# A third staging buffer for output tiles, with another table of places, in a fused attention and two-MLP kernel on one Trainium2 core

## The chip, the cores and the metric

The kernel runs as one program on one core of a Trainium2 chip. The metric is device time in microseconds (us), the median of several executions. The engines that work here are TensorE (PE, with its weight loads as PEld), VectorE (DVE), ScalarE (ACT) and GpSimd (POOL). SyncE (SP) issues most of the transfers, ScalarE the rest.

## The reference

Attention over 4 batches of 12 heads, 448 positions and 64 columns is followed by two small networks with gates made by a convolution over the positions. Everything is float32; the weights arrive as 64-bit words.

```python
# attention, (4, 12, 448, 64)
q_n, k_n = rmsnorm(q, g_q), rmsnorm(k, g_k)
scores = q_n @ k_n.T / sqrt(64); scores -= scores.max(-1)
attn = exp(scores); attn /= attn.sum(-1) + 1e-9
x = attn @ v                                  # heads joined: (4, 448, 768)
# first network, 768 -> 1024 -> 768, 3-tap convolution over positions
h = relu(x @ w_in)                            # (4, 448, 1024)
x = (h * sigmoid(conv3(h))) @ w_out
# second network, 768 -> 768 -> 768, causal 5-tap convolution
val = x @ w_val
out = (sigmoid(conv5(x)) * val) @ w_out2
```

## The kernel before

Every matrix product with float32 accuracy is made of three float16 matmuls: each operand is held as a high and a low half, and high times high, low times high and high times low are summed in PSUM. Attention goes by pairs of heads: rows of q and k are normed, split into halves and turned by transposing transfers (`qa`, `ka`), scores are made in PSUM (`ps`), the row maxima taken (`mx`), exponentials written as float32 (`p32`), split into halves (`p16`), turned again (`pt`) and multiplied with the split values (`vv`, `vm`). The networks use 448 columns per matmul, six or eight blocks of 128 rows deep. Their gates are sums over `scr` tiles on VectorE. Batches follow each other in a pipeline, so attention of a later batch runs beside the networks of an earlier one.

The weights of the second network's last product (`in_moe2_w_out_dram`; the profile leaves numbers in names out and prints `in_moe_w_out_dram`) are fetched in pieces of 128 rows as 64-bit words into slots of the general area `act`. `weight_piece` has a fetch (one transfer) and a split: one ScalarE operation and three VectorE ones that turn the words into float32 (`act<-act`), a ScalarE copy to float16 (`w2<-act`), and a subtraction on GpSimd or VectorE for the low half (`w2<-act,w2`).

An output tile is 128 positions by 384 columns: 18 matmuls (`ps<-act,w2`, in `out_tile`) fill a PSUM bank, `evac` takes the next of `NOSB` buffers `osb` in turn, ScalarE copies the bank into it with a factor, and a transfer stores it in memory. There are 28 such copies, seven for a batch, and 32 stores. Two of the `osb` buffers also serve the gains of the norm at the start (`load_g`).

The order of the instructions is not that of the code. A `Plan` object records every operation (`add`) with the engines that could do it, its dependencies, and the event time at which the code asked for it. `order` gives each a priority `first`: its event time and the length of the work behind it, weighed by `URGENT`, plus a number of the table `OFFSETS` for the event that it belongs to; the lowest goes first. `forward` then lays the operations on the engines by its own model of durations, four passes with `backward` between them, and picks the engine for those that have a choice: a store for example goes to SP's or to ScalarE's queue, a split of weights to one of two engines. `emit` issues the result, so all operations have the line of `emit` (L500) in the profile. Each engine works through its list strictly in order: an instruction that waits holds all those behind it on that engine, and a transfer that SP cannot issue yet holds the transfers behind it.

Of the kernel before, what the change touches and what calls it, by code (L numbers as in the profile page):

```python
# [503 lines left out]
def kernel(  # L504
# [28 lines left out]
    NT = B * S  # L533
    KC = 4
    KR = S // KC
    NQ = 4 * FULL + 2
    NKA = 2
    NV = 4
    NOSB = 2
    NP32 = 2  # L540
    NP = 2
    NTK = 1
    NTQ = 1
    NSCR = 4
    NX16 = 1
# [1357 lines left out]
```

## Time and profile before

| what | value |
|---|---|
| three executions | 618.48, 616.82, 614.95 us; median 616.82 |
| profiled execution | 614.43 us, span 612.6 us |
| granted TensorE clock, mean over the span | 0.997 |
| busy: PE, DVE, ACT, POOL | 588.7 (96%), 483.8 (79%), 413.8 (68%), 270.8 (44%) us |
| chain that ended last, share by engine | PE 70%, DVE 14%, ACT 5%, DMA 4%, issue 3%, POOL 2% |
| bytes moved, mean | 82.09 MB, 134 GB/s |

The span runs from the first to the last instruction of the trace; the profiled execution is 1.8 us longer. All times in the rows below count from the span's start. The share of busy time is a mean over the span, and the stretches of it have different limits, so rows are read by stretch.

### The profile page before, as it was taken

How to read it: one execution, taken by the hardware profiler on the slowest of the kernel's cores; microseconds unless marked ns; L12 is line 12 of the kernel's file. 1: busy time of each engine (PE TensorE's matmuls, PEld its weight loads, DVE VectorE, ACT ScalarE, POOL GpSimd, SP SyncE). 2: the span in 40 equal slices, each digit the busy share in tenths (PEclk: the TensorE clock that was granted, in tenths of full speed). 3: DMA queues.
4: the chain of work that ended last, by engine and by line, in shares of the span. 5: the costliest groups of instructions: out<-in, count | busy, mean ns of one | idle time of the engine just before them, and what ended most of it. 6: DMA issues, size and time to landing. Idle time of an engine off the chain costs nothing.

```text
span 612.6 us, 12783 instructions
## 1 busy us (share of the span) xinstructions
PE 588.7 (96%) x4747; PEld 344.4 (56%) x4747; DVE 483.8 (79%) x1145; ACT 413.8 (68%) x796; POOL 270.8 (44%) x301
## 2 busy tenths in 40 slices
PE   5989899998999999899999999999999999999997
PEld 2767686554666554455555556555455565555554
DVE  6899998989999998898699884499997743397720
ACT  4978999998879986796567663878775543263221
POOL 2254746675556865577375751636661200000000
PEclk9998999999999999999999999999999999999999
DMA  8772758887638879986977867956665675000002
GB/s 207 182 174 62 215 174 205 175 185 170 148 102 226 162 160 166 204 197 105 213 137 144 148 130 181 167 108 112 124 96 111 105 140 119 14 1 1 1 13 78
DMA packets 230803, 82.09 MB, mean 134 GB/s; under 512 B 216863, under 2 KB 226645, under 8 KB 230741
## 3 DMA queue, kind: packets, MB, share of 16 engines
q1 hardware_dynamic: 229413, 79.51, 61.9%
q10 hardware_dynamic: 1328, 1.77, 1.2%
q8 instruction: 37, 0.61, 0.4%
q14 instruction: 25, 0.20, 0.1%
HBM read 38.59 MB, written 5.51 MB: 72 GB/s over the span
## 4 chain that ended last, share of the span: by engine, by line
PE 70%; DVE 14%; ACT 5%; DMA 4%; issue 3%; POOL 2%; SPq 1%; DVEq 0%; ACTq 0%; POOLq 0%
PE ps L500 70%; DVE act L500 3%; DVE w L500 3%; DVE ps L500 3%; DMA act<-in_moe_w_out_dram 2%; DVE scr L500 2%; ACT act L500 1%; DVE half L500 1%; DVE ssq L500 1%; ACT p L500 1%; DMA w<-in_moe_w_out_dram 1%; DMA ka<-tk 1%; SPq L500 1%; DVE root L500 1%; ACT w L500 1%
## 5 line engine op out<-in xcount | busy, mean ns | idle before, releaser
L500 DVE TENSOR_SCALAR_CACHE_REDUCE ps<-ps,root 128x448 f32<-128x448 f32 x168 | 109.4, 687 | 24.6 <-PE ps L500 23.4
L500 PE MATMUL ps<-act,wo 128*128 128x448 f16 x576 | 123.1, 353 | 1.1 <-DVE act L500 1.1
L500 PE MATMUL ps<-act,wi 128*128 128x448 f16 x576 | 117.9, 353 | 4.1 <-DVE scr L500 2.4
L500 ACT ACTIVATE p<-ps,mx 128x448 f32<-128x448 f32 x154 | 91.3, 633 | 27.6 <-DVE mx L500 11.8
L500 POOL TENSOR_TENSOR p<-p,p 128x896 f16<-128x896 f32 x40 | 76.5, 1915 | 65.5 <-ACT p L500 51.7
L500 PE MATMUL ps<-act,wv 128*128 128x448 f16 x432 | 90.3, 353 | 0.3 <-DVE act L500 0.3
L500 PE MATMUL ps<-w,act 128*128 128x384 f16 (+1 forms) x576 | 88.5, 326 | 0.4 <-ACT osb L500 0.4
L500 PEld LDWEIGHTS <-wo 128*128 128x128 f16 x576 | 55.6, 99 | 52.5 <-issue 8.2
L500 PEld LDWEIGHTS <-wi 128*128 128x128 f16 x576 | 54.1, 98 | 54.3 <-issue 8.5
L500 PE MATMUL ps<-ka,qa 64*128 64x448 f16 (+3 forms) x512 | 81.1, 418 | 0.8 <-ACT ka L500 0.7
L500 PE MATMUL ps<-vv,pt 128*128 128x65 f16 (+5 forms) x1440 | 80.0, 205 | 0.2 <-ACT pt L500 0.2
L500 ACT ACTIVATE act<-ps 128x448 f16<-128x448 f32 (+4 forms) x89 | 46.8, 532 | 42.1 <-DVE ps L500 21.9
L500 PEld LDWEIGHTS <-act 128*128 128x128 f16 (+1 forms) x576 | 48.5, 101 | 33.4 <-issue 5.0
L500 PEld LDWEIGHTS <-wv 128*128 128x128 f16 x432 | 40.5, 98 | 38.8 <-issue 4.6
L500 DVE SCALAR_TENSOR_TENSOR act<-ps,cw,act 128x446 f32<-128x446 f32 (+3 forms) x96 | 62.0, 674 | 0.3
L500 PEld LDWEIGHTS <-pt 128*128 128x128 f16 (+1 forms) x1344 | 51.4, 101 | 17.5 <-issue 6.4
L500 ACT ACTIVATE p<-p 128x896 f16<-128x896 f32 x56 | 53.4, 953 | 0.5
L500 DVE SCALAR_TENSOR_TENSOR w<-w 128x768 uint32<-128x768 uint32 (+1 forms) x56 | 47.1, 846 | 0.1
L500 DVE SCALAR_TENSOR_TENSOR scr<-ps,cw,scr 128x447 f32<-128x447 f32 x64 | 41.7, 675 | 1.2 <-ACT scr L500 0.8
L500 DVE SCALAR_TENSOR_TENSOR act<-ps,act 128x448 f16<-128x448 f32 x48 | 29.6, 619 | 6.5 <-ACT act L500 6.4
L500 ACT ACTIVATE osb<-ps 128x384 f32<-128x384 f32 x28 | 13.6, 491 | 30.6 <-PE ps L500 23.7
L500 ACT ACTIVATE ps<-ps 128x448 f32<-128x448 f32 x32 | 16.5, 538 | 25.3 <-PE ps L500 25.3
(131 smaller groups left out, 914.2 us busy)
## 6 DMA issues: line engine op xcount, KB each, us to landing
w<-in_moe_w_in_dram SPq DMA_DIRECT2D x8, 768.0 KB, 6.1
w<-in_moe_w_out_dram SPq DMA_DIRECT2D x8, 768.0 KB, 5.0
kin<-in_k_dram SPq DMA_DIRECT2D x24, 224.0 KB, 3.8
qin<-in_q_dram SPq DMA_DIRECT2D x36, 128.0 KB, 3.4
act<-in_moe_w_out_dram SPq DMA_DIRECT2D x12, 384.0 KB, 4.3
w<-in_moe_w_val_dram SPq DMA_DIRECT2D x12, 384.0 KB, 3.3
vst<-in_v_dram SPq DMA_DIRECT2D x16, 224.0 KB, 3.6
out_dram<-osb SPq DMA_DIRECT2D x17, 192.0 KB, 2.2
```

The lines of the kernel that those rows point to most:

```text
L500: getattr(getattr(nc, e), method)(*a, **k)
```

## The change

`NOSB` goes from 2 to 3, so that the copies of output tiles take three buffers in turn. The table `OFFSETS` is replaced by a longer one with other numbers. Nothing is computed differently: the 6842 recorded operations are the same.

```diff
 OFFSETS = {
...
+    33: -3.36, 38: 0.13, 40: 0.12, 41: 0.12, 42: 0.12, 43: 0.12, 49: 0.56, 56: -0.57, 59: 4.29, 60: 0.25, 61: -2.33, 62:
+    0.25, 63: 0.25, 82: 0.32, 93: -0.21, 94: -0.21, 97: -1.15, 102: 1.97, 106: 0.29, 107: -0.72, 112: -1.3, 115: -5.28,
...
 }
...
     NKA = 2
     NV = 4
-    NOSB = 2
+    NOSB = 3
     NP32 = 2
```

The third buffer shifts by one the numbers behind the names of tiles made later (`ps_116` before is `ps_117` now, `mx2_102` is `mx2_103`). The instructions of both orders stand at the same places, but for swaps over a few places, up to about 238 us of the run before. Behind that they differ on every engine, and both the table and the third buffer have a part in that. VectorE has 977 operations before and 970 now, ScalarE 806 and 810, SP issues 307 transfers and now 311, the matmuls are the same ones.

The first place is ScalarE at 238 us. The rows are its list, before and now; `act_82<-act_82` is a weight piece in conversion, `p32_0` holds the exponentials of scores.

```order
L500 ACTIVATE mx2_102<-mx2_102 128x2
L500 ACTIVATE rs1_110<-ps_116 128x6
L500 ACTIVATE act_82<-act_82 128x384
L500 ACTIVATE p32_0_88<-ps_116,mx2_102 128x448 x2
L500 ACTIVATE p32_1_89<-ps_116,mx3_103 128x448
L500 ACTIVATE p16_0_90<-p32_0_88 128x896
```
```order
L527 ACTIVATE mx2_103<-mx2_103 128x2
L527 ACTIVATE rs1_111<-ps_117 128x6
L527 ACTIVATE vv3_73<-vst1_79 128x7x64
L527 ACTIVATE p32_0_88<-ps_117,mx2_103 128x448 x2
L527 ACTIVATE act_82<-act_82 128x384
L527 ACTIVATE p16_0_90<-p32_0_88 128x896
```

The conversion of the weight piece stood ahead of the exponentials and now stands behind them; the split of a value tile (`vv3`) came to its place.

The second place is VectorE at 249 to 257 us. `scr` are the gate sums of the first network, and the row `scr2_96<-scr2_96,ps_116` (now `ps_117`) is the product of a finished gate with its PSUM tile.

```order
L500 SCALAR_TENSOR_TENSOR scr2_96<-ps_116,cw1_113,scr2_96 128x447
L500 TENSOR_SCALAR act_82<-act_82 128x384
L500 SCALAR_TENSOR_TENSOR scr2_96<-ps_116,cw1_113,scr2_96 128x447
L500 SCALAR_TENSOR_TENSOR scr0_94<-ps_116,cw1_113,scr0_94 128x447
L500 SCALAR_TENSOR_TENSOR scr1_95<-ps_116,cw1_113,scr1_95 128x447
L500 SCALAR_TENSOR_TENSOR scr2_96<-scr2_96,ps_116 128x448
L500 SCALAR_TENSOR_TENSOR act_82<-act_82 128x384
```
```order
L527 SCALAR_TENSOR_TENSOR scr2_96<-ps_117,cw1_114,scr2_96 128x447
L527 SCALAR_TENSOR_TENSOR scr0_94<-ps_117,cw1_114,scr0_94 128x447
L527 SCALAR_TENSOR_TENSOR scr2_96<-ps_117,cw1_114,scr2_96 128x447
L527 SCALAR_TENSOR_TENSOR scr0_94<-ps_117,cw1_114,scr0_94 128x447
L527 SCALAR_TENSOR_TENSOR scr1_95<-ps_117,cw1_114,scr1_95 128x447
L527 SCALAR_TENSOR_TENSOR scr2_96<-scr2_96,ps_117 128x448
```

The conversions of the weight piece (`act_82<-act_82`) left the place ahead of that product.

SP's list at the same time: transfers that turn tiles, and weight pieces from memory.

```order
L500 DMA_TRANSPOSE pt0_92<-p16_0_90 128x14x128
L500 DMA act_82<-in_moe2_w_out_dram 128x768
L500 DMA_TRANSPOSE pt1_93<-p16_1_91 128x14x128
L500 DMA_TRANSPOSE ka1_67<-tk0_86 128x8x112
L500 DMA act_82<-in_moe2_w_out_dram 128x768
```
```order
L527 DMA_TRANSPOSE pt0_92<-p16_0_90 128x14x128
L527 DMA_TRANSPOSE ka1_67<-tk0_86 128x8x112
L527 DMA_TRANSPOSE pt1_93<-p16_1_91 128x14x128
L527 DMA act_82<-in_moe2_w_out_dram 128x768 x2
L527 DMA kin1_84<-in_k_dram 112x8x64
```

The turning of keys (`ka1`) and of probabilities (`pt1`) now stands ahead of the weight piece that was between them. ScalarE's operation that converts this piece moved with it, to seven places further back.

The third place is SP at 268 to 283 us: the last two weight pieces.

```order
L500 DMA act_82<-in_moe2_w_out_dram 128x768
L500 DMA_TRANSPOSE act_82<-x16_0_80 128x3x128
L500 DMA_TRANSPOSE pt0_92<-p16_0_90 128x14x128
L500 DMA_TRANSPOSE act_82<-x16_0_80 128x3x128
L500 DMA act_82<-in_moe2_w_out_dram 128x768
L500 DMA_TRANSPOSE pt1_93<-p16_1_91 128x14x128
L500 DMA out_0_dram<-osb0_98 128x384
```
```order
L527 DMA_TRANSPOSE act_82<-x16_0_80 128x3x128 x2
L527 DMA_TRANSPOSE pt0_92<-p16_0_90 128x14x128
L527 DMA out_0_dram<-osb0_98 128x384
L527 DMA act_82<-in_moe2_w_out_dram 128x768
L527 DMA_TRANSPOSE pt1_93<-p16_1_91 128x14x128
L527 DMA act_82<-in_moe2_w_out_dram 128x768
L527 DMA vst0_78<-in_v_dram 128x7x64
```

Both weight pieces moved back: the first behind three turning transfers and a store, the last behind the turning of probabilities `pt1`.

## Rows read from the trace of the kernel before

**Rows 1.** Windows: us busy, instructions of PE, PEld, DVE, ACT, POOL; clock, DMA.
```profile
240.00:270.00 30.00, 27.89 (x213) 14.84 (x211) 25.63 (x54) 25.11 (x51) 19.40 (x17) 1.00 0.92 191
270.00:300.00 30.00, 29.55 (x286) 16.87 (x284) 24.22 (x56) 18.80 (x40) 21.59 (x19) 1.00 0.83 167
...
360.00:390.00 30.00, 30.00 (x301) 17.73 (x294) 16.32 (x47) 16.97 (x33) 11.15 (x10) 1.00 0.81 175
...
570.00:600.00 30.00, 30.00 (x170) 16.49 (x169) 12.89 (x22) 6.30 (x12) 0.00 (x0) 1.00 0.04 14
```
**Rows 2.** Chain that ended last, its end: start us, us, what.
```profile
291.31 117.58 PE ps L500 x1056
...
508.12 101.07 PE ps L500 x661
...
609.25 0.49 ACT osb L500
```
**Rows 3.** Tile osb: its instructions, and waits at it (us, times).
```profile
L500 ACT ACTIVATE osb<-ps x28: 469/491/515, 270.6 to 609.3; 128x384 f32<-128x384 f32 x28
...
  DMA out_dram<-osb: 6.8, 3
...
  ACT p L500: 2.4, 1
```
**Rows 4.** Timeline of PE: start, us, instruction, count, idle before and releaser.
```profile
239.71 3.19 PE L500 MATMUL ps<-act,wi 128*128 128x448 f16 x16 [1.33 <-ACT p L500]
...
254.49 0.35 PE L500 MATMUL ps<-act,wi 128*128 128x448 f16 x1 [1.77 <-DVE scr L500]
...
261.05 1.48 PE L500 MATMUL ps<-act,wi 128*128 128x448 f16 x7 [0.34 <-DVE scr L500]
...
287.71 3.15 PE L500 MATMUL ps<-w,act 128*128 128x384 f16 x20
291.31 0.97 PE L500 MATMUL ps<-w,act 128*128 128x384 f16 x5 [0.45 <-ACT osb L500]
```
**Rows 5.** Timeline of ACT, 238 to 258 us.
```profile
238.59 0.54 ACT L500 ACTIVATE act<-act 128x384 f32<-128x384 f32 x1 [0.77 <-DMA act<-in_moe_w_out_dram]
239.04 1.67 ACT L500 ACTIVATE p<-ps,mx 128x448 f32<-128x448 f32 x3
...
251.18 0.55 ACT L500 ACTIVATE act<-act 128x384 f32<-128x384 f32 x1 [1.28 <-DMA act<-in_moe_w_out_dram]
...
257.43 0.58 ACT L500 ACTIVATE scr<-scr 128x448 f32<-128x448 f32 x1
```
**Rows 6.** Timeline of DVE, 249 to 259 us.
```profile
251.77 0.36 DVE L500 TENSOR_SCALAR act<-act 128x384 uint32<-128x384 uint32 x1 [1.28 <-ACT act L500]
...
258.04 0.62 DVE L500 SCALAR_TENSOR_TENSOR scr<-scr,ps 128x448 f32<-128x448 f32 x1 [0.30 <-ACT scr L500]
```
**Rows 7.** Timeline of SP's queue, 246 to 283 us.
```profile
246.88 1.07 SPq L500 DMA_DIRECT2D act<-in_moe_w_out_dram  x1
...
250.27 1.67 SPq L500 DMA_TRANSPOSE ka<-tk  x1
...
275.90 0.34 SPq L500 DMA_DIRECT2D act<-in_moe_w_out_dram  x1
280.96 1.54 SPq L500 DMA_TRANSPOSE pt<-p  x1
```
**Rows 8.** Timeline of DVE, 282 to 288 us.
```profile
283.11 1.87 DVE L500 TENSOR_TENSOR half<-half,ssq 128x30 f32<-128x30 f32 x1
...
287.23 0.18 DVE L500 TENSOR_TENSOR half<-half,ssq 128x30 f32<-128x30 f32 x1
287.34 0.56 DVE L500 SCALAR_TENSOR_TENSOR act<-act 128x384 uint32<-128x384 uint32 x1
```
**Rows 9.** Timeline of ACT, 279 to 288 us.
```profile
279.77 0.54 ACT L500 ACTIVATE act<-act 128x384 f32<-128x384 f32 x1
...
287.93 0.52 ACT L500 ACTIVATE w<-act 128x384 f16<-128x384 f32 x1 [4.19 <-DVE act L500]
```

195 rows, old and new, of the table OFFSETS are left out of this document.

## The prediction

> **What bounds the kernel now.** I read the busy time by engine first, and then did not trust it: PE is busy 96% of the span, but a mean over stages hides where the other 4% lie. The windows come next [rows 1]. In 240 to 270 us PE works 27.89 of 30 us, in 270 to 300 us 29.55, and in the windows at 360 and at 570 us all 30. The chain that ended last says the same from the other end [rows 2]: from 291.31 us on its pieces are PE alone (the first has 1056 matmuls in 117.58 us, the last 661 in 101.07), up to the last copy of an output tile at 609.25. So behind 291 us the kernel is as long as its matmuls, and a change of order can only add to it; ahead of 291 us there is idle time of PE that an order could take away. The diff and the lists leave everything ahead of about 238 us as it was. What is left are four gaps of PE between 238 and 292 us [rows 4]: 1.33 us behind an exponential, 1.77 and 0.34 behind gate products of VectorE, 0.45 behind a copy of an output tile. Together 3.89 us, 0.6% of 614.43: this is all that the change can win on PE's own path, unless matmuls of the same set ran faster in another sequence.
>
> **The third buffer.** ScalarE waits for an `osb` buffer to be stored three times, 6.8 us, and an exponential once behind such a wait, 2.4 us [rows 3]; 9.2 us of waiting is what a third buffer could remove. They lie near 380 and 600 us, in the two windows where PE worked 30.00 of 30 us [rows 1]. PE did not feel them: other banks were free and other matmuls ready. So I cost the third buffer at nothing; the cover is PE's queue of matmuls, and if it were gone the wait itself, 2 to 3 us each time, would be the price. The copies of output tiles run from 270.6 us on [rows 3], so of the four gaps only the last one can have to do with them. The Trainium skill's page "Trainium Kernel Development and Optimization", section Best Practices, asks for double buffers so that transfers run beside computing. By that rule, read as "one more buffer where a buffer is waited for", the 9.2 us would come out as time; the window rows show PE without a gap there, so the trace speaks against that here.
>
> **The first place, ScalarE at 238 us.** Before, the conversion of a weight piece starts at 238.59 after 0.77 us of waiting for its transfer, and the exponentials queue behind it until 239.04; PE waits for them until 239.71 [rows 4, 5]. Now a split of a value tile, which waits for no transfer, stands there, and takes about as long as the conversion did (0.54). The exponentials start earlier by the wait, 0.77. Of the 1.33 us gap 0.77 goes. Bounds: 0, if the split has a wait that the trace doesn't show, and 1.33.
>
> **The second place, VectorE at 251 us.** Before, the conversion of a weight piece on VectorE waits 1.28 us for ScalarE, which itself waited 1.28 us for the transfer [rows 5, 6], and the gate product behind it is what PE waits 1.77 us for [rows 4]. Now the conversion stands behind the product, so this gap goes, and the one of 0.34 at 261.05 with it: 2.11. But SP's list is changed too, and here something is given back. The piece was issued at 246.88 and ScalarE could convert it at 251.18, 4.30 later. Now two turning transfers go first; the later of them ended at 250.27 + 1.67 = 251.94 before [rows 7], behind the piece's own 1.07, so the piece is issued at 251.94 - 1.07 = 250.87 and can be converted at 255.17. On ScalarE five instructions, the conversion among them, then stand ahead of the next tanh of a gate (`scr<-scr`, 257.43 before). Instructions of this kind follow each other every 0.45 us (238.59 to 239.04), so the tanh comes at 255.17 + 5 x 0.45 = 257.42, as late as before, and the gate product behind it, at 258.04 before, no earlier [rows 5, 6]. Queued behind the waiting conversion are the gates, and PE waits for them. A new wait of about 2.1 us takes the place of the old one. I keep the 0.34 of the gap at 261.05, since the conversions that stood ahead of that product are now in the wait. So the two places give between 0.34 (the gates hold PE again) and 0.77 + 2.11 = 2.88 (they don't); I take 0.77 + 0.34 = 1.1, near the lower end.
>
> **The third place, SP at 276 us.** The last weight piece was issued at 275.90; now it stands behind the turning of probabilities, which SP issued at 280.96 and held for 1.54 [rows 7], because its source came late. So the piece goes out at 282.5, 6.6 us later. With the 4.30 above it can be converted at 286.8. Then come ScalarE's 0.54 [rows 9], three operations of VectorE of 0.36 to 0.56 (1.48 together) [rows 6, 8] and ScalarE's copy of 0.52: ready at 289.3. Before, it was ready at 287.93 + 0.52 = 288.45 [rows 9], and the run of 20 matmuls at 287.71 [rows 4] went straight through, so PE had no time to spare behind it. That is 0.9 us later than before. The turning itself moves up with the 0.3 to 1.1 us won ahead of it, so against before the piece is 0.6 late at most, and 0.2 early at best. ScalarE's copy of an output tile, for which PE waited 0.45 at 291.31, is now due while PE waits for the weight, so those 0.45 are absorbed.
>
> On VectorE the same subtraction on 30 columns took 1.87 us at 283.11 and 0.18 at 287.23 [rows 8]; the stretch has long GpSimd instructions. The Trainium skill, "SBUF — State Buffer", section on two separate sides, says VectorE and GpSimd share a pair of ports as an exclusive lock, the loser blocked for the whole instruction. By it, the three moved VectorE operations could each be stretched; the sum above takes the short ones.
>
> **Behind 291 us.** The lists differ here too, and I cannot follow every place. PE has no gap, so there is nothing to win. What a wrong place can cost is bounded by a stretch that has gaps: 30 - 27.89 = 2.11 us in one window [rows 1]. I take 0 and keep 2.11.
>
> **The sum.** If the last piece comes in time, the gain is 1.1 + 0.45 = 1.55; if it is late, PE is where the piece lets it be: 0.6 late less the absorbed 0.45, a loss of 0.15 that can grow to 0.6 where the 0.45 is not absorbed. Between -1.55 and +0.6 I take -0.5. The profiled execution took 614.43 (span 612.6), so 613.9 for one like it. The median of the three runs, 616.82, is 2.4 above that execution; the change should shift both alike: 616.3.
>
> **The rivals.**
> 1. All gaps go: the late weight pieces land in the shadow of other work, and PE is gap-free from 238 us on. 616.82 - 3.89 = 612.9. For it: every one of the four gaps has its cause moved in the lists. Against it: the piece at 250 us and the last piece stand later on SP, by 4 and 6.6 us.
> 2. Slower: the last weight piece decides. Its VectorE operations fall beside GpSimd's long instructions, and one is stretched by 1.87 - 0.18 = 1.69, nothing of the earlier gain survives, and the piece is ready 0.9 + 1.69 = 2.6 late, with PE idle for it; 616.82 + 2.6 = 619.4. If the copy of an output tile that is queued on ScalarE behind the conversion then holds a PSUM bank as well, add the 0.45 again: 619.9. It decides from the point where the copy to `w` ends after 288.45 by more than what PE has won. For it: it was ready just in time before. Against it: two of the three VectorE rows there are short ones [rows 8].
> 3. The third buffer does pay: ScalarE's 9.2 us come out, 607.6. Against it is the full PE in both windows.
> 4. Nothing happens: the gains at 238 and 251 us are given back to the last tenth, 616.8. It lies inside the forecast's range.
>
> **How the numbers follow.** Forecast 0.53 (rival 4 included), all gaps gone 0.25, slower by the last piece or a place behind 291 us 0.20, third buffer 0.02. A change of 0.5%, 3.1 us, is about what a measurement of this kernel can tell from none, so faster means under 613.7 and slower over 619.9. Faster: most of the second case (0.22 of 0.25) and the third buffer, 0.24. Slower: half of the 0.20 and a little of the forecast's own tail, 0.12. Same: 0.64. The forecast's own range, with half of the runs' spread (614.95 to 618.48) about it, is 614.5 to 618.2. The range of 8 in 10 takes in the other two: from just below 612.9 to 619.8.
>
> **What would show it right or wrong.** PE's gap at 239 us is shorter by 0.77. The gap at 254 us is gone, and a new one of about 2 us stands near 256 to 258 behind VectorE's gate product, which itself follows a ScalarE conversion waiting for a piece of `w_out`. Near 288 us PE waits for ScalarE's copy `w<-act`. ScalarE's waits for `osb` fall from 6.8 us to near 0 without a change in PE's windows. Wrong would be: a gap-free PE from 238 to 292 us (rival 1), several gaps behind 291 us, or another rate of matmuls in the windows where PE is full.

## The result, and the profile after

The changed kernel takes 620.23 us (median of 10 runs, 613.58 to 629.21), the kernel before 615.39 (10 runs beside it, 613.07 to 619.07). The ratio is 1.0065, with a 95% interval of 1.0039 to 1.0091: slower by 0.65%, just above the range that was forecast, and on the other side of its middle. The forecast started from 616.82, the median of three of these ten runs of the kernel before. The longest run of the changed kernel was a disturbed one and is left out of the ratio.

The timeline of PE in the changed kernel: start, duration, instruction, count, and in brackets the idle time before it with what ended it. These are all the gaps behind 238 us that the profile marks, to be read against [rows 4].

```profile
240.46 3.56 PE L527 MATMUL ps<-act,wi 128*128 128x448 f16 x18 [0.37 <-ACT p L527]
...
259.82 0.76 PE L527 MATMUL ps<-ka,qa 64*64 64x448 f16 x6 [1.60 <-DVE scr L527]
...
271.81 1.32 PE L527 MATMUL ps<-ka,qa 64*128 64x448 f16 x6 [1.87 <-DVE x L527]
...
296.01 0.34 PE L527 MATMUL ps<-vm,pt 128*128 128x130 f16 x3 [0.70 <-DMA pt<-p]
```
```profile
357.66 0.54 PE L527 MATMUL ps<-act,wv 128*128 128x448 f16 x2 [0.17 <-DVE act L527]
...
522.10 0.35 PE L527 MATMUL ps<-vm,pt 128*128 128x130 f16 x3 [0.24 <-DMA pt<-p]
```

The gap behind the exponential fell from 1.33 to 0.37 us, and the ones at 254 and 261 us are gone. Two new ones stand at 259.82 and 271.81, 1.60 and 1.87 us. The second is where the forecast had none. Its releaser is the `x` tile of VectorE. The timelines of VectorE and of GpSimd at that place:

```profile
268.39 0.55 DVE L527 CAST x<-ps 128x384 f16<-128x384 f32 x1
268.85 2.44 DVE L527 SCALAR_TENSOR_TENSOR act<-act 128x384 uint32<-128x384 uint32 x1
271.21 0.55 DVE L527 TENSOR_TENSOR x<-ps,x 128x384 f16<-128x384 f32 x1
```
```profile
268.49 0.55 POOL L527 TENSOR_SCALAR act<-act 128x384 f32<-128x384 f32 x1
268.99 1.88 POOL L527 TENSOR_TENSOR p<-p,p 128x896 f16<-128x896 f32 x1
```

A weight conversion of VectorE (`act<-act`, 384 columns) lasts 2.44 us. An instruction of this form takes 0.56 in [rows 8]. It stood beside the end of a short GpSimd instruction and beside the split of probabilities behind that, which lasted until 270.87, and the second half of the `x` tile that PE needs stood behind it. Over the whole program the instructions of this form became longer, as the lines grouped by form show, first of the kernel before, then of the changed one (busy us, mean ns of one):

```profile
L500 DVE SCALAR_TENSOR_TENSOR act<-act 128x384 uint32<-128x384 uint32 x24 | 15.1, 638 | 1.4 <-POOL act L500 1.4
```
```profile
L527 DVE SCALAR_TENSOR_TENSOR act<-act 128x384 uint32<-128x384 uint32 x24 | 20.0, 837 | 0.6 <-POOL act L527 0.4
```

The 24 instructions of this form need 4.9 us more; 1.88 of them are this one's. Behind the gap the clock fell too. Windows of 2 us of the changed kernel (us busy of PE, PEld, DVE, ACT, POOL; then the granted clock, DMA share, GB/s):

```profile
270.00:272.00 2.00, 0.19 (x2) 0.10 (x2) 2.00 (x3) 0.70 (x3) 0.95 (x2) 1.00 0.39 73
272.00:274.00 2.00, 2.00 (x9) 0.70 (x7) 2.00 (x7) 1.90 (x4) 1.56 (x3) 0.72 0.32 66
274.00:276.00 2.00, 2.00 (x6) 0.73 (x5) 2.00 (x5) 1.78 (x4) 1.75 (x3) 0.50 0.63 124
276.00:278.00 2.00, 2.00 (x26) 1.34 (x25) 2.00 (x4) 1.42 (x3) 0.78 (x1) 0.93 1.01 235
```

PE worked 0.19 of 2 us, and in the next 4 us it was granted 0.72 and 0.50, that is the lower of its levels (1.2 of 2.4 GHz) for most of them. In the window 270 to 300 us of before the clock was 1.00 [rows 1].

The account of the two profiled executions: the span grew from 612.6 to 617.6, by 5.0 us. The matmuls behind the first gap start at 240.46 against 239.71, 0.75 later although their gap is 0.96 shorter, so 1.7 us of the 5.0 were lost ahead of the first place that the change touches. They belong to that execution: its clock was 0.89 from 60 to 90 us, which is 3.3 us, while the trace of before has 0.94 from 30 to 60 us, 1.8 us. 3.3 us of the 5.0 are left. The gaps behind 238 us add up to 0.37 + 1.60 + 1.87 + 0.70 + 0.17 + 0.24 = 4.95 us against 3.89: 1.1. From 270 to 300 us the mean clock was 0.94, which is 30 x 0.06 = 1.8 us:

```profile
270.00:300.00 30.00, 27.48 (x254) 15.48 (x253) 25.42 (x52) 19.71 (x40) 20.34 (x20) 0.94 0.66 136
```

That makes 2.9 of 3.3; 0.4 us I could not place.

### The profile page after: what moved, and what is told of

Same layout as the page of the kernel before. It is cut to its first block, busy times and chain, and to the rows that moved or that the text cites. A ratio compares the mean times of both kernels' runs of the same rounds, so it can differ in the third digit from the quotient of the medians.

```text
span 617.6 us, 12804 instructions
## 1 busy us (share of the span) xinstructions
PE 592.0 (96%) x4747; PEld 346.1 (56%) x4747; DVE 487.2 (79%) x1138; ACT 416.9 (68%) x804; POOL 270.1 (44%) x300
## 4 chain that ended last, share of the span: by engine, by line
PE 63%; DVE 15%; ACT 8%; DMA 8%; issue 3%; POOL 2%; SPq 0%; ACTq 0%; DVEq 0%; POOLq 0%
PE ps L527 63%; DVE act L527 4%; DVE ps L527 4%; ACT p L527 2%; DMA pt<-p 2%; DVE w L527 2%; ACT act L527 2%; DMA ka<-tk 1%; DMA act<-in_moe_w_out_dram 1%; DMA w<-in_moe_w_in_dram 1%; DVE ssq L527 1%; ACT w L527 1%; DMA w<-in_moe_w_out_dram 1%; DVE half L527 1%; DVE tq L527 1%
## 5 line engine op out<-in xcount | busy, mean ns | idle before, releaser
L527 PE MATMUL ps<-act,wi 128*128 128x448 f16 x576 | 119.8, 356 | 0.7 <-ACT p L527 0.4
L527 DVE SCALAR_TENSOR_TENSOR act<-ps,cw,act 128x444 f32<-128x444 f32 (+3 forms) x96 | 63.1, 675 | 0.6
L527 DVE SCALAR_TENSOR_TENSOR w<-w 128x768 uint32<-128x768 uint32 (+1 forms) x56 | 45.4, 817 | 0.1
L527 PEld LDWEIGHTS ps<-vv,pt 128*128 128x128 f32 (+1 forms) x288 | 33.6, 185 | 1.2 <-issue 0.7
L527 PE MATMUL ps<-vm,pt 128*128 128x130 f16 (+3 forms) x240 | 28.5, 238 | 4.8 <-ACT pt L527 3.8
```

Of the source, the lines that this page charges most:

```text
L527: getattr(getattr(nc, e), method)(*a, **k)
```

## The experiments

Each kernel was timed in five rounds beside the kernel before. Those that move instructions do it behind the planner, on its finished lists, and nothing else changes. The numbers in `MOVES` are places in the planner's record of operations:

```diff
+    # (x, y, s): x goes right behind (s = 1) or ahead of (s = 0) y, on y's engine
+    MOVES = [...]
     def emit(self, nc):
```

**nosb3_old**, the third buffer with the old table.

```diff
-    NOSB = 2
+    NOSB = 3
```

> The third buffer with the old table. In its lists the stretch from 238 to 283 us (the split of a value tile ahead of the exponentials, the weight pieces behind the turning transfers, the weight conversion ahead of the x tile on VectorE) stands as in the changed kernel. Theory A, the loss comes from that stretch: the long VectorE act<-act of about 2.4 us beside GpSimd's p<-p,p near 270 us, a PE gap of 1.5 to 2 us behind it, a lower granted clock for some us after it; time as the changed kernel or worse, 619 to 622. Theory B, the loss comes from the new numbers of the table behind 291 us: this kernel is as fast as the one before, 614 to 617.

**nosb2_new**, the new table with two buffers: the changed kernel with

```diff
-    NOSB = 3
+    NOSB = 2
```

> Two buffers with the new table. Its lists from 238 to 283 us are nearly those of the kernel before: the x tile on VectorE is ahead of the weight conversion, the weight pieces on SP are early. Theory A: no PE gap above 1 us near 270 us, no fall of the clock there, 614 to 617. Theory B (the numbers of the table are the loss): 619 to 621.

Measured: 625.76 us, ratio 1.0175 (1.0131 to 1.0219), and 628.68 us, ratio 1.0205 (1.0168 to 1.0243). Both halves of the change are worse than the whole, and neither theory has it right: the gap near 270 us, by which they were to be told apart, is in neither. With the old table VectorE has the conversion at the same place of its list as the changed kernel, but there it takes 0.76 us and PE waits 0.20; with the new table alone PE waits 0.17. Each has gaps that the two full kernels lack. The largest of the old table with three buffers is 1.67 us, at 283.75; that of the new table alone:

```profile
419.28 6.95 PE L527 MATMUL ps<-act,wi 128*128 128x448 f16 x27 [3.93 <-DVE act L527]
```

The gaps behind 238 us add up to 6.90 and 10.40 us. What they have above the 3.89 of the kernel before is under a third of the one loss and about half of the other; the rest I did not place. Buffers and table do not add up: the planner lays its lists by dependencies, a third buffer takes some away, and the lists shift from 238 us on, 32 us ahead of the first copy of an output tile [rows 3]. Each table does worse with the other's number of buffers.

**x_first**, the weight conversion that took 2.44 us goes behind the `x` tile and two gate products.

```diff
+    MOVES = [(2499, 2857, 1)]
```

> The changed kernel with one VectorE instruction moved: the weight conversion that took 2.44 us at 268.85 goes behind the x tile and the two gate products that follow. Theory A: the x tile is done by 269.6 instead of 271.76, the PE gap of 1.87 us at 271.81 shrinks to under 0.4, and the clock does not fall at 273 us, which saves about 1.6 us more; 620.2 becomes 616 to 617.5. If the gap goes but the clock falls all the same, 618.5. If the gap is only handed on to the next weight tile, no change, 620.

Measured: 620.26 us, ratio 1.0055 (1.0019 to 1.0091). The gap of 1.87 us is gone, but the time is not won. The profile shows a loss again 85 us later. First PE, then VectorE, then GpSimd:

```profile
353.13 0.35 PE L547 MATMUL ps<-act,wv 128*128 128x448 f16 x1
356.78 0.54 PE L547 MATMUL ps<-act,wv 128*128 128x448 f16 x2 [3.30 <-DVE act L547]
```
```profile
345.95 4.19 DVE L547 TENSOR_SCALAR ssq<-ssq 128x30 f32<-128x30 f32 x1
```
```profile
345.55 1.15 POOL L547 TENSOR_TENSOR tq<-tq 128x448 f32<-128x448 f32 x1
346.64 1.90 POOL L547 TENSOR_TENSOR p<-p,p 128x896 f16<-128x896 f32 x1
348.48 1.02 POOL L547 TENSOR_TENSOR vv<-vst,vv 128x448 f16<-128x448 f32 x1
349.43 1.55 POOL L547 TENSOR_TENSOR tq<-tq 128x224 f32<-128x224 f32 x3
```

An operation on 30 columns of sums of squares (`ssq<-ssq`, called the 30-column sum below) stays 4.19 us on VectorE, from 345.95 to 350.14, while GpSimd works without a pause through three instructions into a fourth. PE then waits 3.30 us. In the changed kernel's own profile the same operation, at 350.03, takes 0.99 us, and PE waits 0.17 behind it, at 357.66. The clock falls again behind the long wait:

```profile
354.00:356.00 2.00, 0.00 (x0) 0.00 (x0) 1.86 (x9) 1.87 (x5) 0.00 (x0) 1.00 1.05 198
...
358.00:360.00 2.00, 2.00 (x13) 0.92 (x10) 1.84 (x8) 0.58 (x1) 0.00 (x0) 0.52 0.56 123
360.00:362.00 2.00, 2.00 (x24) 1.41 (x22) 0.67 (x5) 1.88 (x3) 1.30 (x2) 0.63 1.01 190
```

**pool_late**, GpSimd's split of probabilities goes behind the next low half of a weight; VectorE's list is that of the changed kernel.

```diff
+    MOVES = [(3057, 2501, 1)]
```

> The changed kernel with one GpSimd instruction moved: the split of probabilities (p<-p,p, 1.88 us at 268.99) goes behind the following low half of a weight. VectorE's list is untouched. Theory A, the conversion is long because the GpSimd instruction runs beside it: VectorE's act<-act near 269 us takes 0.55 to 0.7 us instead of 2.44, and the PE gap falls as in the run with the moved conversion; 616 to 618. Rival, VectorE's instruction is long for another reason (its source comes late): it stays at 2.4 us and the time at 620.

Measured: 618.65 us, ratio 1.0042 (1.0011 to 1.0072). VectorE and GpSimd at the place:

```profile
268.25 0.78 DVE L547 SCALAR_TENSOR_TENSOR act<-act 128x384 uint32<-128x384 uint32 x1
268.95 0.54 DVE L547 TENSOR_TENSOR x<-ps,x 128x384 f16<-128x384 f32 x1
```
```profile
268.07 0.55 POOL L547 TENSOR_SCALAR act<-act 128x384 f32<-128x384 f32 x1
...
270.83 1.89 POOL L547 TENSOR_TENSOR p<-p,p 128x896 f16<-128x896 f32 x1
```

The conversion takes 0.78 us with its own list unchanged, since GpSimd's split now starts at 270.83. So the long conversion is GpSimd's doing. This run too has the 4.2 us sum near 347 us and a PE gap of 3.38 us behind it, which eats the gain.

**ssq_pool**, the sum on 30 columns goes to GpSimd, where the kernel before has it.

```diff
+    MOVES = [(4061, 4649, 1)]
```

> The changed kernel with one operation on another engine: a sum on 30 columns (ssq<-ssq), which took 0.99 us on VectorE at 350.03 in its profile and 4.19 us in the run with the x tile first, goes to GpSimd, where the kernel before had it. Theory A (VectorE loses to GpSimd's long instructions at two places, 269 and 346 us): the gap behind VectorE's act near 357 us never appears, the one at 271 us stays; 618 to 620. Rival, the place at 346 us was an accident of the moved instructions: 620, as the changed kernel.

Measured: 617.31 us, ratio 1.0026 (0.9993 to 1.0058). The gap at 271 us stayed (1.98 us); PE's list has none near 357 us. The interval overlaps that of the changed kernel, so this run alone does not show that the sum costs anything there.

**x_and_ssq**, both edits.

```diff
+    MOVES = [(2499, 2857, 1), (4061, 4649, 1)]
```

> Both edits: the weight conversion behind the x tile, and the 30-column sum on GpSimd. Theory A: neither the gap of 1.87 us at 271.8 nor the one of 3.30 at 356.8 is left, and the clock does not fall behind them; what is left is the 1.2 to 1.6 us at 259 us; 615 to 616.5. Rival, the time lost is handed on again to a third place: 618 or more.

Measured: 616.73 us, ratio 1.0013 (0.9979 to 1.0047). Its profile has neither a gap behind the `x` tile nor one near 357 us. With both places mended the kernel cannot be told from the one before. The intervals of this and of the changed kernel overlap between 1.0039 and 1.0047 only; the middle moved by 0.5%, 3.2 us.

**piece_first**, the weight piece on SP goes ahead of the turning of keys again, and **all_three**, this with both other edits.

```diff
+    MOVES = [(2367, 2708, 0)]                                        # piece_first
+    MOVES = [(2499, 2857, 1), (4061, 4649, 1), (2367, 2708, 0)]      # all_three
```

> The changed kernel with one transfer moved on SP: the weight piece that stood behind the turning of keys and of probabilities is issued ahead of the turning of keys again, as in the kernel before. Prediction's second place: the PE gap of 1.60 us at 259.82 behind the gate product goes, and with the piece's conversion earlier VectorE's act<-act no longer meets the x tile at 269 us, so that gap goes too; 616 to 618. Rival, the wait only moves to the turned keys, which now go out later: a gap of about 1 us ahead of the score matmuls, 619.5 to 620.5.

> The two edits, and the weight piece ahead of the turning of keys as well. Theory A: PE has no gap above 0.7 us behind 239 us, and the gain that was forecast as the best case is there; 613 to 615, faster than the kernel before. Rival, the later turning of keys costs as much as the earlier piece gives: 615 to 616.5.

Measured: 618.25 us, ratio 1.0036 (1.0000 to 1.0072), and 616.25 us, ratio 1.0010 (0.9978 to 1.0041). The wait of 1.60 us at 259 us is the piece's: with the piece early it is gone or 0.37 us. But the turned keys now come late, 0.90 and 1.11 us of PE. The best case of 613 to 615 is missed; in all_three time is handed on once more, to a copy of an output tile that waits for its buffer:

```profile
250.21 0.74 PE L548 MATMUL ps<-ka,qa 64*128 64x448 f16 x6 [1.11 <-DMA ka<-tk]
...
256.53 0.76 PE L548 MATMUL ps<-ka,qa 64*64 64x448 f16 x6 [0.37 <-DVE scr L548]
...
390.65 2.24 PE L548 MATMUL ps<-act,wi 128*128 128x448 f16 x11 [2.48 <-ACT osb L548]
```
```profile
388.89 0.49 ACT L548 ACTIVATE osb<-ps 128x384 f32<-128x384 f32 x1 [1.37 <-DMA out_dram<-osb]
```

**piece_and_ssq**, the early piece and the sum on GpSimd, with the conversion ahead of the `x` tile.

```diff
+    MOVES = [(4061, 4649, 1), (2367, 2708, 0)]
```

> The changed kernel with the weight piece ahead of the turning of keys and the 30-column sum on GpSimd; the weight conversion stays ahead of the x tile. In the run with the piece alone the gap at 270 us was 0.54 us without moving the conversion. Theory A: as fast as the run with all three edits or faster, 614.5 to 616.5. Rival, the 269 us place needs its own edit: 617 to 618.

Measured: 619.33 us, ratio 1.0051 (1.0019 to 1.0082). The gap behind the `x` tile, 0.54 us in piece_first, is 2.29 here with the same lists at that place. VectorE and GpSimd, first in piece_first, then here:

```profile
269.03 1.11 DVE L548 SCALAR_TENSOR_TENSOR act<-act 128x384 uint32<-128x384 uint32 x1
```
```profile
269.18 0.58 POOL L548 TENSOR_SCALAR act<-act 128x384 f32<-128x384 f32 x1
269.73 2.16 POOL L548 TENSOR_TENSOR p<-p,p 128x896 f16<-128x896 f32 x1
```
```profile
268.50 2.87 DVE L548 SCALAR_TENSOR_TENSOR act<-act 128x384 uint32<-128x384 uint32 x1
```
```profile
268.56 0.57 POOL L548 TENSOR_SCALAR act<-act 128x384 f32<-128x384 f32 x1
269.06 1.90 POOL L548 TENSOR_TENSOR p<-p,p 128x896 f16<-128x896 f32 x1
```

In piece_first the conversion ends soon after GpSimd's short instruction, and it is the split that is longer; here it ends only behind the split. No run shows what decides between the two, and the place needs its own edit.

**before_plus**, the kernel before with three conversions moved back by hand.

```diff
+    MOVES = [(2315, 2546, 1), (2413, 2690, 1), (2414, 2659, 1)]
```

> The kernel before (two buffers, old table) with three conversions of weight pieces moved back by hand, and nothing else: on ScalarE one behind the exponentials at 239 us and one behind the tanh at 253 us, on VectorE its next step behind the gate product at 253.8. The transfers stay where they were. It takes from the change what the prediction counted as its gains at the first and second place, without the weight pieces that SP sends later. Prediction's terms: PE gaps of 1.33 and 1.77 us go to about 0.1 and 0.2; 2 to 3 us faster than before, 612 to 613.5. Rival, the conversions meet GpSimd's long instructions a few us later and the gain is given back: 615 to 617.

Measured: 614.65 us, ratio 1.0001 (0.9965 to 1.0036). The gap at 239 us is gone, the one of 1.77 us is down to 1.02, and a new one stands a few us later:

```profile
251.94 0.35 PE L521 MATMUL ps<-act,wi 128*128 128x448 f16 x1 [1.02 <-DVE scr L521]
...
257.50 0.76 PE L521 MATMUL ps<-ka,qa 64*64 64x448 f16 x10 [1.32 <-DVE scr L521]
...
259.83 1.49 PE L521 MATMUL ps<-act,wi 128*128 128x448 f16 x7 [0.34 <-DVE scr L521]
```

From 238 to 262 us PE's gaps were 1.33 + 1.77 + 0.34 = 3.44 us [rows 4] and are 1.02 + 1.32 + 0.34 = 2.68 now: of the 2 to 3 us expected 0.76 is left, which this measurement cannot tell from nothing.

**before_ssq**, the kernel before with the 30-column sum on VectorE.

```diff
+    MOVES = [(4061, 4060, 1)]
```

> The kernel before with one operation moved to the other engine: the sum on 30 columns at 352.81 us goes from GpSimd to VectorE, behind the sum of the keys' squares, as the changed kernel has it. Theory A (VectorE is kept out by GpSimd's instructions there): the operation takes 1 to 4 us instead of 0.2, and where that is over 3 PE gets a gap behind it; 616 to 619. Rival, it is short and the time unchanged, 615 to 616: then the long one belongs to the changed order around it.

Measured: 618.42 us, ratio 1.0021 (0.9985 to 1.0057). In the profile the sum takes 0.98 us and PE waits 0.26 behind it. Inconclusive: it is not the 0.2 us of GpSimd and not the 4.19 of x_first, and the time cannot be told from that of the kernel before.

**old_order_4buf**, the lists of the kernel before word for word, with four buffers.

```diff
-    NOSB = 2
+    NOSB = 4
...
     def emit(self, nc):
+        # the order of the other kernel: op numbers by engine
...
```

> The kernel before with its instruction lists kept word for word on every engine, and four staging buffers (three would not do: two copies stand out of turn in these lists, and with three they would share a buffer). It tells the buffers apart from the order. The prediction's step: ScalarE's waits for an osb buffer (6.8 us, and 2.4 behind one) go to near 0, PE's gaps stay, and the time stays at 615 to 616. Rival (the third buffer pays by itself): up to 9 us faster, 607 to 611. Other rival (more buffers cost, through their place in memory or the stores' timing): over 618.

Measured: 615.61 us, ratio 1.0020 (0.9987 to 1.0052). PE's four gaps are the old ones. ScalarE's waits for a buffer:

```profile
  DMA out_dram<-osb: 4.1, 1
```

6.8 us became 4.1, and no time came out.

**gates_first**, the two edits, and two late weight conversions behind the tanh and the gate product of 259 us.

```diff
+    MOVES = [(2499, 2857, 1), (4061, 4649, 1),
+             (2413, 2724, 1), (2496, 2413, 1), (2414, 2725, 1), (2415, 2414, 1)]
```

> The changed kernel with the weight conversion behind the x tile and the 30-column sum on GpSimd, and also the two weight conversions that wait for late transfers moved behind the tanh and the gate product near 259 us, on ScalarE and on VectorE. Theory A: the gap of 1.3 to 1.6 us at 259 us goes, which was the prediction's new wait; 614.5 to 615.5 against 616.7 of the run with the two edits. Rival: the conversions then come too late for VectorE or meet GpSimd, and the time is handed on; 616.5 to 618.5.

Measured: 615.72 us, ratio 1.0027 (1.0002 to 1.0052). The wait at 259 us is gone, and what replaces it is small:

```profile
261.42 0.34 PE L548 MATMUL ps<-vm,pt 128*128 128x130 f16 x3 [0.41 <-DMA pt<-p]
...
263.75 0.32 PE L548 MATMUL ps<-w,act 128*128 128x384 f16 x1 [0.68 <-ACT p L548]
```

Its time is not below that of x_and_ssq: what the gates gave does not show at the end. No kernel here beats the one before.

## Why the prediction was wrong

- **What bounds the kernel.** Right as far as the runs go: no kernel here is faster than the one before, and the windows behind 300 us stayed nearly full. Wrong in one point: behind 291 us I took 0 and kept 2.11 us as the end. The changed kernel has 0.70 + 0.17 + 0.24 = 1.11 us of gaps there, and a single wait of 3.30 us near 357 us appeared in x_first, one of 3.38 in pool_late. The stretch without gaps in the trace of before said nothing of how near it was to having one.
- **The third buffer at nothing.** Right for the buffer alone, by old_order_4buf with the order held and four buffers. ScalarE's waits did not go to near 0, as I wrote: the changed kernel still has one of 5.0 us, at 522 us, where PE waits 0.24 us, and for turned probabilities. One of the three waits, 3.07 us until 602.83, lies behind the two windows that I named; PE was busy there as well, until 609.19 [rows 2].
- **The first place.** Right: 0.77 of the gap was to go, 0.96 went.
- **The second place, as far as it went.** Right in kind and nearly in size. The rows of the changed kernel, ScalarE, VectorE, then SP:

```profile
256.21 0.56 ACT L527 ACTIVATE act<-act 128x384 f32<-128x384 f32 x1 [1.58 <-DMA act<-in_moe_w_out_dram]
...
258.55 1.02 ACT L527 ACTIVATE scr<-scr 128x448 f32<-128x448 f32 x2
```
```profile
259.14 0.62 DVE L527 SCALAR_TENSOR_TENSOR scr<-scr,ps 128x448 f32<-128x448 f32 x1 [1.32 <-ACT scr L527]
```
```profile
251.37 1.65 SPq L527 DMA_DIRECT2D act<-in_moe_w_out_dram  x2
```

  The piece was forecast to go out at 250.87 (251.37, in an execution 0.75 late), to be convertible at 255.17 (256.21), the tanh at 257.42 (258.55), and a new PE gap of about 2 us behind the gate product (1.60). all_three and gates_first, where that wait is 0.37 or gone, show that the late conversions are its cause.
- **The step that failed.** "So the two places give between 0.34 (the gates hold PE again) and 0.77 + 2.11 = 2.88 (they don't); I take 0.77 + 0.34 = 1.1, near the lower end." I followed the late piece to the gates that queue behind it and stopped there; the sum has no term for what VectorE does between the second place and the third, and puts it at nothing without a row. The conversion that took 2.44 us is not even one of the late piece. It is the last VectorE step of the next piece, which SP sent at 252.63, 0.60 later than before in an execution 0.75 late. Before, this step ran at 264.51, in a row with two others of its kind; in the new list of VectorE it stands between the two halves of the `x` tile, at 268.85, and there it met GpSimd's split. I wrote down this very mechanism as the second rival, priced at 1.69 us, and put it at the third place, for the last piece only; it struck ahead of that, for 2.44 - 0.56 = 1.88 us, with a lower clock behind it (1.8 us in the profile) that no term of the sum had. x_first and pool_late show it from both engines. By gaps of PE, the first place gave 0.96, the second 2.11 - 1.60 = 0.51, and the 0.45 at 291 us went as forecast; against these 1.92 stand 1.87 for the `x` tile and 1.11 behind 291 us.
- **The engine that an operation runs on.** I counted VectorE's operations (977 and now 970) and did not look at which ones changed sides. The 30-column sum at 350 us came from GpSimd to VectorE. In the changed kernel's profile it cost PE 0.17 us; with the first place mended, in x_first and pool_late, it took 4.19 and 4.20 us. ssq_pool, with it sent back, is at 1.0026 against 1.0065; x_and_ssq with both at 1.0013.
- **The third place.** Half right. The last piece went out late (283.42; 282.5 was forecast), and a conversion there was stretched as well, 2.29 us at 285.77 beside a split of 1.89 at 285.76. PE did not wait near 288 us for it, because it was itself late by then: its first matmul with that piece starts at 293.00, against 288.52 before. The gap of PE that is there is 0.70 us at 296.01, behind turned probabilities.

Shown are the first place of loss, at the `x` tile, and GpSimd's part in it; that the second, at the 30-column sum, costs over 3 us once the first is mended; and that mending both takes the loss away within the measurement. Argued only is what the second costs in the changed kernel itself. The lower clock goes with PE's gap at the `x` tile: behind gaps of 1.87, 1.98 (ssq_pool) and 2.29 us (piece_and_ssq) the next 4 us have a mean of 0.63, 0.67 and 0.64, and in x_first, pool_late, piece_first, all_three and gates_first, with 0.54 or less there, it is 1.00 from 264 to 280 us. A gap alone does not settle it, since the 2.48 us in all_three were not followed by a fall. Left open are 0.4 us of the profile's account, most of the loss in nosb3_old and half of that in nosb2_new, and where the gain of gates_first went.

## What to carry to other kernels

Read every engine's list through the whole stretch that changed, not only where a wait was moved: what now stands ahead of each tile that the bounding engine needs, and what the neighbouring engine does at that moment. Where a planner decides, compare what changes engines, and hold the lists fixed when you want the price of a buffer; here each table of places lost about 2% with the other's number of buffers. A full PE stretch shows that no wait reaches it, not by how much it is spared.

## What the runs showed of the hardware

A VectorE instruction on 30 columns was held 4.19 us while GpSimd worked through several instructions in a row; the same form takes 0.18 at 313.05 us in piece_and_ssq. The Trainium skill's page "SBUF — State Buffer", section on two separate sides, has the two engines share a pair of ports as a lock that is held for the whole instruction. The rows agree that one engine stands while the other works: VectorE's conversion takes 2.44 us beside the split of 1.88, and 0.78 with the split moved away. Either engine can be the one that stands: in piece_first the conversion takes 1.11 us, and the split 2.16 instead of 1.88. In the 4.19 us VectorE was passed over three times in a row.

The spread between runs of one kernel is mostly the clock: the kernel before took 610.72 to 615.10 us in 13 runs at a mean granted clock of 1.000 and 620.29 in one at 0.989, and the one run of the changed kernel at 1.000 took 613.58. With a spread like that a change of 0.5% needed ten runs or more on either side.
